# Dynamic convolution and squared-ReLU FFN on one core: the convolution of blocks 8 to 32 cut into 64-row pieces in two row halves

## Chip, core and metric

The kernel runs on one core of a Trainium2 chip. The time is device microseconds from the first to the last instruction of one execution with what lies around it; the median of three runs before the change is 729.51 us (729.48 to 729.95). One more execution was recorded by the profiler: its span is 728.4 us.

## What is computed

Every token of 8 sequences of 4096 tokens has 192 channels in 8 heads of 24. For each token and head a softmax over 7 generated weights gives the taps of a causal convolution over this token and the 6 before it. The result goes through an FFN of width 2048 with a squared ReLU.

```python
w = softmax(weight_gen, axis=-1)                       # (8, 4096, 8 heads, 7 taps)
x_pad = concatenate([zeros((B, 6, D)), x], axis=1)     # causal
out[b, s, h] = sum over k of w[b, s, h, k] * x_pad[b, s + k, head h]
y = out.reshape(32768, 192)
result = maximum(y @ w_in, 0) ** 2 @ w_out             # 192 -> 2048 -> 192
```

## The kernel before

Tokens are taken in 64 sub-blocks of 512 (`TB`). The first two are blocks of their own, all others go in pairs, so there are 33 blocks (`BLOCKS`, numbered from 0). From block 8 on (`FIRST_SPREAD`) a block's convolution is `st_conv_spread`; these are 25 blocks, sub-blocks 14 to 63.

**Convolution as matmul.** A sub-block is cut into 5 pieces of 128 tokens (`NT`, `STEP` = 104): a piece starts 24 tokens before the first of its 104 new tokens (96 in the last piece), so that the 6 tokens of history lie in it. `x_load` brings the pieces of x with POOL's DMA queue, 128 tokens on partitions, 192 channels wide, casting to fp16 on the way (`block_load`: one transfer for all 5 pieces, two or three where a piece starts elsewhere). `wr_load` brings the softmax weights of the same tokens from a DRAM buffer on SP's queue in the same cut. `st_band` (DVE) multiplies the weights, repeated along the columns, by a 0/1 mask, which gives for each head a band matrix of 128 rows (tokens read) by 104 columns (tokens made). The matmul takes 32 channels of x as weights (128x32) and a head's band as the moving operand (128x104). `st_conv_spread` runs over 4 head pairs k (three pairs of heads, and a fourth slot that holds the heads left over), 5 pieces, 2 sub-blocks (`half`) and 2 heads (`e`): 80 matmuls. The four of (`half`, `e`) go to the four groups of 32 columns of the array (`tile_position=(0, p0)`) and so to four groups of 32 PSUM partitions. Each result tile `yp` holds two k in two PSUM banks of 512 columns, two tiles a block: ACT evicts the first, DVE the second, to `y` in fp16 (L512). Then four small transfers on SP's queue move the rows of the leftover heads to where the FFN wants them (L516).

**FFN.** `st_unit` makes a 128-wide slice of the hidden layer for both halves: 6 matmuls of 64x512, the two 64-row halves of the array at a time (L581). ACT applies the ReLU (L595), DVE squares (L599). `st_mm2` runs one block later: matmuls with 64x128 weights and 192 columns, again two row halves at a time, into two banks (L630); ACT and DVE add the two banks (L644, L646), and SP stores.

**Order.** It is written out by hand. A block's plan (`steady_spread`) is the string `MuMuuu MuMuuu MuCMuuu MuMuuu`: 16 units `u` of this block, 8 half quarters `M` (32 matmuls each) of the second product of the block before, and at `C` the convolution of the next block, followed by the loads of x for the block after that. `B` steps make bands for the next block before units 1 and 5; `S` and `E` steps do a piece of the softmax of a later batch. `load_rows(j + 2)` at the start of a block, or the last `S` of a softmax part, issues the weight loads. On SP's queue these stand between the output stores and the row moves of L516.

**Buffers.** x has 2 (`p_x`, the two sub-blocks of one block), so a load of x waits for the matmuls of the convolution before; weights have 4 (`p_wr`), bands 3 (`p_bd`). Three slots of two PSUM banks (`ps_h`) go round among `yp` and `h`.

Of the kernel before, what the change touches and what calls it, by code (L numbers as in the profile page):

```python
# [9 lines left out]
def kernel(  # L10
# [26 lines left out]
    nc = tc.nc  # L37
    f32 = mybir.dt.float32
    f16 = mybir.dt.float16

    B, S, D = x.shape
    H, KK = weight_gen.shape[2], weight_gen.shape[3]
# [5 lines left out]
    FIRST_SPREAD = 8  # L48
    HP = H // 2

    P = 128
    TB = 512
    NBB = S // TB
    NSUB = B * NBB
    BLOCKS = [(0, 1), (1, 1)] + [(n, 2) for n in range(2, NSUB, 2)]
# [6 lines left out]
    SL = 8  # L62
    RT = 64
    NK = D // RT

    NT = 5
    STEP = 104
    BASE = -24
    starts = [BASE + STEP * i for i in range(NT)]
    bounds = [0, 104, 208, 312, 416, TB]  # L70
    ROW_ORDER = (0, 1, 2, 3, 4)

    AluOp = mybir.AluOpType
    AxisX = mybir.AxisListType.X
# [2 lines left out]
    const = ctx.enter_context(tc.tile_pool(name="const", bufs=1))  # L77
# [5 lines left out]
    p_bd = ctx.enter_context(tc.tile_pool(name="p_bd", bufs=3))  # L83
# [5 lines left out]
    ps_h = ctx.enter_context(tc.tile_pool(name="ps_h", bufs=3, space=bass.MemoryType.PSUM))  # L89
# [6 lines left out]
    w_p = const.tile([P, WQ, 2, NQ + NQ // 2], f16, name="w_p")  # L96
    w_o = const.tile([P, NF, Dm], f16, name="w_o")
    mask = const.tile([P, P, 2], f16, name="mask")
    FIRST = 8
    NSEL = TB + TB - P + FIRST + P  # L100
    sel = const.tile([P, NSEL], f16, name="sel")
    PARTS = {0: (8, 8, 8, 8), 1: (8, 8, 16), 2: (16, 16)}
    v_big = const.tile([P, R + 2 * HALO, HP, SL, 2], f16, name="v_big")
    v_first = [
        const.tile([P, FIRST + 2 * HALO, HP, SL, 2], f16, name=f"v_first{i}") for i in (0, 1)
    ]
# [5 lines left out]
            fill=1.0, base=FIRST - 1, channel_multiplier=FIRST,  # L112
        )

    def band_mask():

        nc.gpsimd.memset(mask, 1.0)
        flat = mask.rearrange("p c e -> p (c e)")
        for sign, base in ((1, 0), (-1, 2 * KK - 1)):
            nc.gpsimd.affine_select(  # L120
                out=flat, in_=flat, pattern=[[sign, 2 * P]], compare_op=AluOp.is_ge,
                fill=0.0, base=base, channel_multiplier=-2 * sign,
            )

# [64 lines left out]
    class Softmax:  # L191
# [10 lines left out]
        def load(self, eng, cuts=None):  # L202
            r, rh = self.r, self.rh
            self.wg = wg = self.tile(p_wg, p_wg, "wg", HK, "wg8").rearrange(
                "p (r h k) -> p r h k", h=H, k=KK
            )
            base = weight_gen[self.b, self.t0 : self.t0 + r]
            n = P if self.t0 + P * r + HALO <= S or self.b < B - 1 else P - 1

            def src(first, count, parts):  # L210
                return bass.AP(
                    tensor=base.tensor, offset=base.offset + first * HK,
                    ap=[[r * HK, parts], [1, count * HK]],
                )

            if n == P:
                cuts = cuts or (0, rh)
                for lo, hi in zip(cuts, cuts[1:]):
                    eng.dma_start(  # L219
                        out=wg[:, lo:hi].rearrange("p r h k -> p (r h k)"),  # L220
                        in_=src(lo, hi - lo, P),
                    )
            else:
                nc.vector.memset(wg[:, r:rh], 0.0)
                eng.dma_start(
                    out=wg[:, 0:r].rearrange("p r h k -> p (r h k)"), in_=src(0, r, P)
                )
                eng.dma_start(
                    out=wg[0:n, r:rh].rearrange("p r h k -> p (r h k)"), in_=src(r, HALO, n)
                )  # L230
# [56 lines left out]
    vd_t = {}  # L287
# [7 lines left out]
    x_t, wr_t, pr_t, bd_t, yp_t, y_t, g_t, gp_t, t1_t, o_t, o_sb_t = ({} for _ in range(11))  # L295
# [12 lines left out]
    def tile_start(j, i):  # L308

        t1 = (j % NBB + 1) * TB  # L310
        return TB - P if i == NT - 1 and t1 in ends(j // NBB) else starts[i]

    def block_load(j, dst, src, width, eng):
        t0 = (j % NBB) * TB
        first, last = int(t0 == 0), NT
        if first:
            eng.dma_start(out=dst[:, 0], in_=src[0:P, :])  # L317
        a = t0 + tile_start(j, NT - 1)
        if a != t0 + starts[-1]:
            last = NT - 1  # L320
            eng.dma_start(out=dst[:, last], in_=src[a : a + P, :])
        ap = rows(src, t0 + starts[first], width)
        ap = bass.AP(
            tensor=ap.tensor, offset=ap.offset,
            ap=[ap.ap[0], [STEP * width, last - first], ap.ap[2]],
        )
        eng.dma_start(out=dst[:, first:last], in_=ap)  # L327

    def x_load(j):
        x_t[j] = p_x.tile([P, NT, D], f16, name="xt")  # L330
        block_load(j, x_t[j], x[j // NBB], D, nc.gpsimd)

    def x_load_f32(j):
# [13 lines left out]
    def wr_load(j):  # L347
        wr_t[j] = p_wr.tile([P, NT, HP, SL * 2], f16, name="wr")
        wr = wr_t[j].rearrange("p t g c -> p t (g c)")
        block_load(j, wr, vd_t[j // NBB], H * SL, nc.sync)  # L350

    def wr_load_sbuf(j, parts, order, engines):

# [15 lines left out]
    def select_rows(j, s, tiles, places):  # L369
# [4 lines left out]
        for m, i in enumerate(tiles):  # L374
# [6 lines left out]
            for r in range(s.r):  # L381
                c = a + FIRST - 1 - r
                nc.tensor.matmul(
# [12 lines left out]
    def st_band(j, tiles):  # L396
# [21 lines left out]
            op=AluOp.mult,  # L418
        )

    quads = []
    for q in range(D // 32):
        ha, hb = (32 * q) // G, (32 * q + 31) // G
# [22 lines left out]
    def st_conv_first(j):  # L446
# [10 lines left out]
        places += [(q, r0 + 32 * (q - 4), 1) for r0 in (0, RT) for q in (4, 5)]  # L457
        for i in ROW_ORDER:
            lo, b = bounds[i], bounds[i + 1]
# [21 lines left out]
    def st_conv_spread(j):  # L481

        s0, n = BLOCKS[j]
        y = p_y.tile([P, NK + 1, TB], f16, name="y")
        y_t[j] = y
        for ks in ((NK, NK - 1), (0, 1)):
            yp = ps_h.tile([P, 2, TB], f32, name="yp", tag="h")
            k0 = min(ks)
            for k in ks:
                for i in range(NT):  # L490
                    a, b = bounds[i], bounds[i + 1]
                    for half in (0, 1):
                        s = s0 + half
                        hi = a + (STEP if tile_start(s, i) == starts[i] else b - a)
                        bd = bd_t[s][:, H * a : H * hi].rearrange(
                            "p (g c e) -> p g e c", g=HP, e=2
                        )
                        for e in (0, 1):
                            head = 2 * k + e
                            p0 = RT * half + 32 * e  # L500
                            c0 = min(G * head, D - 32)
                            nc.tensor.matmul(  # L502
                                out=yp[p0 : p0 + 32, k - k0, a:b],
                                lhsT=x_t[s][:, i, c0 : c0 + 32],
                                rhs=bd[:, head // 2, e, 0 : b - a],
                                start=True,
                                stop=True,
                                skip_group_check=True,
                                tile_position=(0, p0),
                            )  # L510
            copy = nc.vector.tensor_copy if k0 == 0 else nc.scalar.copy
            copy(out=y[:, k0 : k0 + 2], in_=yp)  # L512
        for p0 in range(0, P, 32):
            head = SPREAD + p0 // 32 % 2
            r0 = p0 + G * head - min(G * head, D - 32)
            nc.sync.dma_start(out=y[p0 + G : p0 + 32, 0:NK], in_=y[r0 : r0 + G, NK])  # L516
# [139 lines left out]
        )  # L656

    def st_bands(j):
        first = int(j % NBB == 0)
        last = NT - int(tile_start(j, NT - 1) != starts[-1])  # L660
        split = 2 if j == BLOCKS[NFIRST][0] else first
        for tiles in (range(first), range(first, split), range(split, last), range(last, NT)):
            if tiles:
                st_band(j, tiles)

    with nc.allow_low_precision("fp16 matmul pipeline"), tc.manual_schedule():
# [3 lines left out]
        for b in range(B):  # L670
            t0 = 0
# [29 lines left out]

        s0, s1, s2 = parts[:3]
        spin(46)
        band_mask()
        s0_cuts = (0, FIRST // 2, FIRST, s0.rh)
        s0.load(nc.sync, s0_cuts)
        w_st = p_wg.tile([P, (R + HALO) * HK], f32, name="w_st", tag="wg")[:, 0 : NQ + NQ // 2]
# [14 lines left out]
        o0, o1, ring = (ps_o, "o0"), (ps_o, "o1"), (ps_h, "h")  # L722
        select_rows(0, s0, ROW_ORDER, (o1, ring, ring, ring, o0))
        copy_rows(0, ROW_ORDER[:2])
        x_cast(0, nc.scalar.copy, 1, 3)
        copy_rows(0, ROW_ORDER[2:])
        x_cast(0, nc.scalar.copy, 3, NT)
        for i in ROW_ORDER:
            st_band(0, (i,))
        select_rows(1, s0, ROW_ORDER, (o1,))  # L730
        copy_rows(1, ROW_ORDER, NT)
# [17 lines left out]
        s2.load(nc.gpsimd)  # L749
        x_load(2)  # L750
        nc.gpsimd.memset(v_big, 0.0)

# [12 lines left out]
        fill = {}  # L767
# [22 lines left out]
        for n, s in enumerate(parts):  # L790
            k = n - min(m for m, p in enumerate(parts) if p.b == s.b)
# [4 lines left out]
        for n, s in enumerate(parts[4:], 4):  # L796
            b, f = s.b, s.fb
            k = n - min(m for m, p in enumerate(parts) if p.b == b)
# [8 lines left out]
        for j in range(len(plans), NBLK - 1):  # L807
            a = BLOCKS[j + 1][0]
# [67 lines left out]
        for j in range(NBLK):  # L876
# [6 lines left out]
            for step in plans[j].split():  # L883
                kind, n = step[0], int(step[1:] or 0)
# [26 lines left out]
        j = NBLK - 1  # L911
# [44 lines left out]
```

## Time and profile before

| what | value |
|---|---|
| median of three runs | 729.51 us |
| span of the profiled execution | 728.4 us |
| PE busy | 722.0 us (99%) |
| DVE busy | 625.8 us (86%) |
| ACT busy | 612.0 us (84%) |
| POOL busy | 98.5 us (14%) |
| convolution matmuls of blocks 8 to 32 (L502) | 2000: 1600 of 104 columns, 400 of 96 |
| granted TensorE clock | 1.000 |

A line such as `L502 PE MATMUL yp<-bd,xt 128*32 128x104 f16` names the source line, the engine, the operation, the tile written and the tiles read, the part of the array in use (rows x columns) and the moving operand (partitions x elements). PE's weight loads have a row of their own, PEld; they run beside matmuls. Matmuls overlap one another, and their ends are modelled, so the time that a stretch of matmuls takes is read from the chain of waits, where each piece ends when the next begins, and not from the mean duration of one.

### The profile page before, as it was taken

The numbers are of one execution on the slowest core, as the hardware profiler recorded it, in microseconds if no ns is written. First come the engines' busy times: TensorE is split into PE (matmuls) and PEld (weight loads), VectorE is DVE, ScalarE is ACT, GpSimd is POOL, SyncE is SP. The second block draws the span as 40 slices with busy tenths as digits, with TensorE's granted clock in tenths as the row PEclk, the third lists the DMA queues.
The fourth block names the chain that finished last, engine by engine and source line by source line (L and its number), as shares of the span: only waits on it lengthen the run. The fifth ranks groups of instructions, "written<-read, shape, count | busy, mean of one in ns | idle before, by whom it ended". The sixth has DMA issues, their size and how long they took to land.

```text
span 728.4 us, 31046 instructions
## 1 busy us (share of the span) xinstructions
PE 722.0 (99%) x14078; PEld 530.1 (73%) x14078; DVE 625.8 (86%) x839; ACT 612.0 (84%) x731; POOL 98.5 (14%) x146
## 2 busy tenths in 40 slices
PE   8999999999999999999999999999999999999998
PEld 5668877777777777777777777777777777777777
DVE  7999997998898998888988888988888988778753
ACT  6998888888888888888888888888888888888883
POOL 7231223411001100011001010010000110001000
PEclk9999999999999999999999999999999999999999
DMA  9664465676245443356432554343544325444112
GB/s 193 128 113 106 82 125 89 128 142 138 78 71 133 99 84 68 75 116 125 83 62 58 135 104 88 66 74 110 114 78 87 57 53 117 67 87 77 30 46 67
DMA packets 126272, 68.30 MB, mean 94 GB/s; under 512 B 85353, under 2 KB 122556, under 8 KB 125628
## 3 DMA queue, kind: packets, MB, share of 16 engines
q0 software_dynamic: 46192, 19.43, 22.9%
q1 hardware_dynamic: 79804, 46.79, 22.5%
q8 instruction: 110, 1.80, 1.1%
q14 instruction: 22, 0.18, 0.1%
q10 hardware_dynamic: 144, 0.10, 0.0%
HBM read 50.18 MB, written 28.70 MB: 108 GB/s over the span
## 4 chain that ended last, share of the span: by engine, by line
PE 98%; DMA 1%; SPq 0%; ACT 0%; issue 0%; ACTq 0%
PE o L630 47%; PE h L581 44%; PE yp L502 4%; PE h L566 2%; PE yp L536 1%; DMA w_st<-in_moe_w_in_dram 1%; SPq L219 0%; PE yp L466 0%; ACT w_i L740 0%; SPq L135 0%; SPq L133 0%; ACT y L476 0%; SPq L327 0%; SPq L317 0%; ACT o_sb L644 0%
## 5 line engine op out<-in xcount | busy, mean ns | idle before, releaser
L595 ACT ACTIVATE t<-h 128x1024 f16<-128x1024 f32 x512 | 496.6, 1027 | 60.1 <-PE h L581 58.4
L630 PEld LDWEIGHTS <-g 64*128 64x128 f16 (+1 forms) x8032 | 344.3, 94 | 55.2 <-issue 2.3
L630 PE MATMUL o<-w_o,g 64*128 64x192 f16 (+1 forms) x8032 | 380.1, 243 | 0.1
L599 DVE TENSOR_TENSOR g<-t 128x2048 f16<-128x2048 f16 (+1 forms) x287 | 307.4, 1105 | 28.7 <-ACT t L595 28.3
L581 PE MATMUL h<-y,w_p 64*128 64x512 f16 x2400 | 291.7, 376 | 0.0
L581 PEld LDWEIGHTS <-w_p 64*128 64x128 f16 x2400 | 113.9, 94 | 94.8
L406 DVE TENSOR_TENSOR bd<-wr,mask 128x4160 f16<-128x4160 f16 (+4 forms) x90 | 149.5, 1685 | 1.2 <-ACT wr L391 1.2
L646 DVE TENSOR_TENSOR o_sb<-o,o_sb 128x384 f32<-128x384 f32 x123 | 68.4, 556 | 61.4 <-ACT o_sb L644 60.3
L327 POOL DMA_DIRECT2D xt<-in_x_dram x63 | 52.6, 838 | 415.4 <-PE yp L502 362.5
L644 ACT COPY o_sb<-o 128x384 f32<-128x384 f32 x129 | 61.6, 477 | 45.7 <-PE o L630 44.4
L581 PE MATMUL h<-y,w_i 64*128 64x512 f16 x576 | 70.5, 376 | 0.0
L581 PEld LDWEIGHTS <-w_i 64*128 64x128 f16 x576 | 30.5, 94 | 21.7 <-issue 1.2
L502 PEld LDWEIGHTS <-xt 128*32 128x32 f16 x2000 | 24.6, 95 | 10.6 <-issue 10.6
L266 DVE TENSOR_TENSOR v_big<-ex,rcp 128x112 f16<-128x112 f32 (+5 forms) x180 | 29.9, 237 | 2.1 <-DMA vd<-v_big 1.1
L512 DVE CAST y<-yp 128x1024 f16<-128x1024 f32 x25 | 30.4, 1218 | 0.0
L502 PE MATMUL yp<-bd,xt 128*32 128x104 f16 (+1 forms) x2000 | 28.4, 210 | 0.0
L244 ACT ACTIVATE ex<-wg 128x560 f32<-128x560 f32 (+5 forms) x40 | 26.3, 659 | 1.2 <-DMA wg<-in_weight_gen_dram 1.2
L251 DVE TENSOR_REDUCE ssum<-ex 128x80 f32<-128x560 f32 (+5 forms) x40 | 25.6, 639 | 1.3 <-ACT ex L244 1.3
L512 ACT CAST y<-yp 128x1024 f16<-128x1024 f32 x25 | 25.2, 1007 | 0.0
L258 DVE RECIPROCAL rcp<-ssum 128x64 f32<-128x64 f32 (+4 forms) x39 | 23.0, 589 | 1.4
L317 POOL DMA_DIRECT2D xt<-in_x_dram x7 | 3.9, 555 | 120.4 <-PE yp L502 109.4
L361 POOL DMA_DIRECT2D wr<-v_first x24 | 13.0, 559 | 24.0 <-DVE v_first L266 23.8
(42 smaller groups left out, 111.9 us busy)
## 6 DMA issues: line engine op xcount, KB each, us to landing
out_dram<-o_sb SPq DMA_DIRECT2D x63, 384.0 KB
xt<-in_x_dram POOLq DMA_DIRECT2D x42, 240.0 KB, 4.9
wg<-in_weight_gen_dram SPq DMA_DIRECT2D x4, 1064.0 KB
xt<-in_x_dram POOLq DMA_DIRECT2D x21, 192.0 KB, 5.0
wr<-vd SPq DMA_DIRECT2D x38, 80.0 KB
vd<-v_big SPq DMA_DIRECT2D x5, 512.0 KB
y<-y SPq DMA_DIRECT2D x100, 24.0 KB
wg<-in_weight_gen_dram SPq DMA_DIRECT2D x3, 616.0 KB
```

What stands on the lines that cost most here:

```text
L244: nc.scalar.activation(out=self.ex[:, lo:hi].rearrange("p r g k e -> p (r g) k e"), in_=self.wg[:, lo:hi].rearrange("p r (g e) k -> p (r g ...
L266: eng.tensor_tensor(out=bass.AP(tensor=v.tensor, offset=v.offset + lo * H * SL + lo % SL * 2 + g * SL * 2, ap=[list(v.ap[0]), [H * SL + 2, ...
L327: eng.dma_start(out=dst[:, first:last], in_=ap)
L406: nc.vector.tensor_tensor(out=bd_t[j][:, H * lo : H * (lo + len(tiles) * n)].rearrange("p (g m c) -> p g m c", g=shape[1], c=2 * SL), in0= ...
L502: nc.tensor.matmul(out=yp[p0 : p0 + 32, k - k0, a:b], lhsT=x_t[s][:, i, c0 : c0 + 32], rhs=bd[:, head // 2, e, 0 : b - a], start=True, sto ...
L512: copy(out=y[:, k0 : k0 + 2], in_=yp)
L581: nc.tensor.matmul(out=h[:, half], lhsT=w_in_chunk(w, u, slot, half), rhs=y_t[j][r0 : r0 + RT, k], start=(slot == 0), stop=(slot == NK - 1 ...
L595: nc.scalar.activation(out=t1[:, e], in_=h, func=ActF.Relu)
L599: nc.vector.tensor_tensor(out=g[:, a : e + 1], in0=t1[:, a : e + 1], in1=t1[:, a : e + 1], op=AluOp.mult)
L630: nc.tensor.matmul(out=oo[:, cc * Dm : (cc + 1) * Dm], lhsT=g[r0 : r0 + n, cc * P : (cc + 1) * P], rhs=w_o[r0 : r0 + n, fc, :], start=(fc ...
L644: nc.scalar.copy(out=o_sb, in_=o[0][:, c])
L646: nc.vector.tensor_tensor(out=o_sb, in0=o[1][:, c], in1=o_sb, op=AluOp.add)
```

## The change

Sub-blocks from 14 on (`FIRST_HALF`, the first of block 8) are cut differently. Each is split in two halves of 256 tokens; a half is cut into 5 pieces of 64 tokens, four with 56 new tokens (the piece starts 8 before them) and a last one with 32 (starting 32 before them). The first token half lies on partitions 0 to 63, the second on 64 to 127, so a tile holds 2 x 5 pieces and is as wide as before.

- `half_load` takes the place of `block_load` for x and for the weights: for each half one transfer of 4 pieces and one of the last piece. At the start of a sequence 8 rows are cleared by POOL, and one more transfer is issued.
- `half_bands` takes the place of `st_band`: one DVE operation for the four pieces of 56 columns and one for the piece of 32, on all 128 partitions, with a second mask `mask_half`, which POOL makes at the start.
- `st_conv_spread` issues each matmul twice, once for each half, with 64 rows and half as many columns, at `tile_position=(64 r, p0)`. `yp` is laid out as half, k, column, so that each half has a PSUM bank of its own; the evictions read it in the order k, half, column.

```diff
+    HT = TB // 2
+    FIRST_HALF = BLOCKS[FIRST_SPREAD][0]
+    WSTEP = RT - SL
+    windows = [(WSTEP * i, WSTEP * i - SL) for i in range(HT // WSTEP)]
+    windows.append((WSTEP * len(windows), HT - RT))
+    NW = len(windows)
+    w_ends = [a for a, _ in windows[1:]] + [HT]
...
+    def half_load(j, dst, src, width, eng):
+        t0 = (j % NBB) * TB
+        for r in (0, 1):
+            a, p = t0 + HT * r, RT * r
+            first = int(a == 0)
+            if first:
+                nc.gpsimd.memset(dst[0:SL, 0], 0.0)
+                eng.dma_start(out=dst[SL:RT, 0], in_=src[0 : RT - SL, :])
+            eng.dma_start(
+                out=dst[p : p + RT, first : NW - 1],
+                in_=bass.AP(
+                    tensor=src.tensor, offset=src.offset + (a + windows[first][1]) * width,
+                    ap=[[width, RT], [WSTEP * width, NW - 1 - first], [1, width]],
+                ),
+            )
+            b = a + windows[-1][1]
+            eng.dma_start(out=dst[p : p + RT, NW - 1], in_=src[b : b + RT, :])
...
+    def half_bands(j):
+        bd_t[j] = p_bd.tile([P, H * NT * STEP], f16, name="bd")
+        for lo, hi in ((0, NW - 1), (NW - 1, NW)):
+            a, start = windows[lo]
+            n, shift = w_ends[lo] - a, a - start
+            shape = (P, HP * (hi - lo), n // SL, 2 * SL)
+            nc.vector.tensor_tensor(
+                out=bd_t[j][:, H * a : H * w_ends[hi - 1]].rearrange(
...
+                in1=mask_half[:, shift : shift + n]
...
-            yp = ps_h.tile([P, 2, TB], f32, name="yp", tag="h")
+            yp = ps_h.tile([P, 2, 2, HT], f32, name="yp", tag="h")
             k0 = min(ks)
             for k in ks:
-                for i in range(NT):
-                    a, b = bounds[i], bounds[i + 1]
+                for (a, _), b, i in zip(windows, w_ends, range(NW)):
                     for half in (0, 1):
...
-                            nc.tensor.matmul(
-                                out=yp[p0 : p0 + 32, k - k0, a:b],
-                                lhsT=x_t[s][:, i, c0 : c0 + 32],
-                                rhs=bd[:, head // 2, e, 0 : b - a],
...
-                                tile_position=(0, p0),
-                            )
+                            for r in (0, 1):
+                                nc.tensor.matmul(
+                                    out=yp[p0 : p0 + 32, r, k - k0, a:b],
+                                    lhsT=x_t[s][RT * r : RT * (r + 1), i, c0 : c0 + 32],
+                                    rhs=bd[RT * r : RT * (r + 1), head // 2, e],
...
+                                    tile_position=(RT * r, p0),
+                                )
             copy = nc.vector.tensor_copy if k0 == 0 else nc.scalar.copy
-            copy(out=y[:, k0 : k0 + 2], in_=yp)
+            copy(
+                out=y[:, k0 : k0 + 2].rearrange("p k (r c) -> p k r c", r=2),
+                in_=yp.rearrange("p r k c -> p k r c"),
+            )
...
     def st_bands(j):
+        if j >= FIRST_HALF:
+            return half_bands(j)
...
         nc.gpsimd.memset(v_big, 0.0)
+        band_mask(mask_half, RT)
```

`x_load` and `wr_load` call `half_load` from sub-block 14 on, and `band_mask` takes the mask and its number of rows as arguments.

## Prediction

> **What bounds the kernel now.** First the page: busy times, the chain that ended last, and the queue that brings instructions.
>
> ```profile
> PE 722.0 (99%) x14078; PEld 530.1 (73%) x14078; DVE 625.8 (86%) x839; ACT 612.0 (84%) x731; POOL 98.5 (14%) x146
> ...
> q8 instruction: 110, 1.80, 1.1%
> ...
> PE 98%; DMA 1%; SPq 0%; ACT 0%; issue 0%; ACTq 0%
> PE o L630 47%; PE h L581 44%; PE yp L502 4%; PE h L566 2%; PE yp L536 1%; DMA w_st<-in_moe_w_in_dram 1%; SPq L219 0%; PE yp L466 0%; ACT w_i L740 0%; SPq L135 0%; SPq L133 0%; ACT y L476 0%; SPq L327 0%; SPq L317 0%; ACT o_sb L644 0%
> ```
>
> PE alone sets the end: it is 98% of the chain, and no wait for another engine has a share. So the change is worth what it takes from, or adds to, PE's own stream. Whether that stream is bound by columns is read from the chain of waits in a steady stretch.
>
> ```profile
> 392.91 1.94 PE h L581 x18
> 394.86 1.32 PE o L630 x32
> 396.18 0.65 PE h L581 x6
> 396.82 1.08 PE yp L502 x68
> 397.90 1.43 PE o L630 x32
> ```
>
> L581 and L630 run two at a time: 1.94/9 = 215.6 ns a pair of 512 columns, 1.32/16 = 82.5 ns a pair of 192. The line through both is 0.416 ns a column and 2.6 ns a matmul, for each part of the array that works by itself. For the convolution, four at a time, it gives 45.9 ns for a round of 104 columns and 42.5 for 96. A block has 4 k x (4 + 1) rounds: 16 x 45.9 + 4 x 42.5 = 904 ns.
>
> A steady block takes 22.09 us from one convolution to the next (first matmuls at 374.67 and 396.75 in the timeline). 48 pairs of L581 and 128 of L630 are 10.35 + 10.56 = 20.91, so 1.18 us are left for the convolution: 904 ns of columns and 0.27 us around them (the change of tile shape on both sides, the first weight load, jitter). The convolution is bound by columns as well, not by issuing.
>
> Third, the groups with shapes kept apart, for prices:
>
> ```profile
> L406 DVE TENSOR_TENSOR bd<-wr,mask 128x4160 f16<-128x4160 f16 x41 | 94.9, 2316 | 0.0
> ...
> L327 POOL DMA_DIRECT2D xt<-in_x_dram x63 | 52.6, 838 | 415.4 <-PE yp L502 362.5 <-PE yp L536 42.5 <-issue 9.9
> ...
> L406 DVE TENSOR_TENSOR bd<-wr,mask 128x3328 f16<-128x3328 f16 x21 | 39.5, 1882 | 0.0
> ...
> L502 PE MATMUL yp<-bd,xt 128*32 128x104 f16 x1600 | 27.3, 211 | 0.0
> ...
> L317 POOL DMA_DIRECT2D xt<-in_x_dram x7 | 3.9, 555 | 120.4 <-PE yp L502 109.4 <-PE yp L536 11.0
> ```
>
> **PE, the part that counts.** Removed per block: 80 weight loads and 80 matmuls in 20 rounds of four, 904 ns. Added: 160 and 160 in 20 rounds of eight. The 0.27 us around them I leave: the neighbours keep their shapes.
> By columns, a round of 56 takes 0.416 x 56 + 2.6 = 25.9 ns, one of 32 takes 15.9: 16 x 25.9 + 4 x 15.9 = 478 ns, a gain of 426 ns a block, 10.7 us in 25 blocks.
> A round now has 16 instructions, and no row shows PE taking 16 in 26 ns. The nearest short row is the first round of a convolution, a stretch of 14 ns (396.750 to 396.764) with L502's instructions alone:
>
> ```profile
> 396.75:396.76 0.01, 0.01 (x4) 0.01 (x4) 1.00 0.46 55
> ```
>
> Four matmuls and four loads begin in it: 1.75 ns an instruction, so 28 ns for a round of 16, whatever its width. 20 x 28 = 560 ns, a gain of 344 ns a block, 8.6 us in all. The nearest long row is L536 in the window from 48 to 53 us, where 240 instructions take 1.50 us of the chain: 6.25 ns each; but columns bind there too, so it says only that PE can do this much. At that pace 320 instructions take 2.00 us: 1.10 us lost a block, 27.4 us in all. The ends are -10.7 and +27.4 us. I take 28 ns a round: it is PE's own measured pace where nothing but issuing binds, and between a floor of 25.9 and a stream never seen at its limit it is the nearest row.
>
> The Trainium skill (TensorE: Matmul & The Clock Gate, "Wait — 56ns, not 53.3ns?") says that starts are never under about 25 ns apart, however few the columns. Over the whole array 160 matmuls would then need 4.0 us a block; the trace has 80 in 1.08 us, 13.5 ns apart, so the rule can hold at most for each tile. There it would lift the 32-column rounds from 15.9 to 25 ns, an estimate of 514 ns for the block's columns, still under 560.
>
> **DVE.** Rows of 4160 and 3328 elements give 0.522 ns an element and 146 ns a call. Two calls of 1792 and 256 elements: 1081 + 280 = 1.36 us in place of 2.32. Over 50 sub-blocks DVE is busy some 48 us less. Worth nothing: DVE is in no share of the chain. Evictions keep their element counts (ACT 1007 ns, DVE 1218 ns) and read the same banks.
>
> **POOL and x.** Per block 8 transfers in place of 2 to 4, of as many rows. Each 0.56 (L317) to 0.84 us (L327): 4.4 to 6.7 us from the end of the convolution (first issue at 376.10), and 5.0 us, at most 8.0, to landing. Done by 391; needed at 396.75. Cost nothing, covered by the block's 22 us; without this cover every block would wait. The new mask is five small POOL operations at the start, ahead of a load of x that waits for a convolution anyway; the clearing of 8 rows of x waits where its load would.
>
> **SP and the weights.** Also 8 issues in place of 2 or 3. In a steady block they begin at 384.12, and behind them stands an output store that waits for DVE until 394: at L327's median of 0.51 us they end at 388.2. Covered; the row moves of L516, which the next block's first L581 needs, stand before them. At the start of a sequence it is tighter:
>
> ```profile
> 245.14 2.83 SPq L516 DMA_DIRECT2D y<-y  x4
> 248.58 0.34 SPq L280 DMA_DIRECT2D vd<-v_big  x1
> 252.11 0.35 SPq L317 DMA_DIRECT2D wr<-vd  x1
> 252.51 0.97 SPq L327 DMA_DIRECT2D wr<-vd  x2
> 253.59 0.47 SPq L651 DMA_DIRECT2D out_dram<-o_sb  x1
> ```
>
> From 248.92 SP waits for the store to DRAM; then come 9 loads, not 3. The first band of that sub-block is made at 256.17. Its five loads are issued by about 252.1 + 5 x 0.51 = 254.7, and POOL's rows put 3.9 to 5.0 us to landing: DVE may wait up to 3.5 us, some five times in the run. Behind that band stand squares, which the second product needs one block later, and ACT has three buffers of two units ahead. Cost nothing; if the cover failed, 5 x 3.5 = 17 us at most.
>
> **Sum.** 729.5 - 25 x 0.344 = **720.9 us** (the profiled span, 728.4, lies 1.1 us under the median; I take the change from the median).
>
> **Rivals.**
> *Instructions don't come fast enough (slower).* Place: PE's stream in L502. 1.80 MB in 110 packets are 256 instructions of 64 bytes each; 1.1% of 16 engines x 728.4 us over 110 is 1.17 us a packet, 4.6 ns an instruction. A convolution is now 320 instructions in a row, more than a packet. If what is fetched and decoded ahead doesn't carry it, 320 x 4.6 = 1.47 us against 0.904: 0.57 x 25 = +14 us, 743.6. It decides from 904/320 = 2.8 ns an instruction on. For it: today nothing in the trace runs under 5.6 ns for longer than a round. Against it: fetching averages 18% of one engine, and the short row shows 1.75.
> *Gain partly returned.* The same supply at about 2.3 ns: 736 ns a block, -4.2 us, 725.3.
> *Only four at once.* If tiles in the same 32 columns but other row halves take turns: 40 rounds, 32 x 25.9 + 8 x 15.9 = 956 ns, +1.3 us, 730.8: the change doesn't do what it says. For it: no row runs both splits together. Against it: L581 runs row halves and L502 column groups together, each at its line.
> *A transfer is late.* x or the weights arrive after the matmul or band that needs them. At 1 us a block +16, 746. The margins above (5.7 us for x) speak against it.
>
> **Chances.** Forecast (717.9 to 723) 0.48; partly returned (723 to 728) 0.14; four at once 0.10; instruction supply 0.22; transfers 0.06. A measurement here can tell about 0.2% from no change, 1.5 us: 728.0 and 731.0. Faster 0.62; same takes half of four at once, 0.05, and 0.01 of the edges; slower 0.32. The low end is the column floor, 729.5 - 10.7 = 718.8, less 1.3 for switches that may get cheaper between kin shapes: 717.5. The high end takes four at once and the supply rival up to 3.9 ns: 738. Left out are some 0.17. The forecast's own range is 717.9 to 723.
>
> **What would show it.** L502: 4000 matmuls, and per block in the chain 0.65 to 0.8 us in place of 1.08; steady blocks 21.75 us apart. DVE's band rows 1.08 and 0.28 us. POOL's wait for L502 shorter by some 3 us a block, and no PE wait for a transfer of x. I am wrong if the convolution takes over 1.0 us, or if PE shows waits at L502's first matmuls or inside L630 after it.

## The result, and the profile after

| | before | after |
|---|---|---|
| median, four runs each on one chip | 729.73 us (729.48 to 730.99) | 757.65 us (756.0 to 757.89) |
| ratio of the times | 1 | 1.0374, 95% interval 1.0359 to 1.0388 |
| span of the profiled execution | 728.4 us | 755.8 us |

The change makes the kernel 28 us slower; 720.9 was forecast. The page of the changed kernel, in its parts for busy time, DMA queues and the chain that ended last:

```profile
PE 734.2 (97%) x16078; PEld 543.7 (72%) x16078; DVE 579.5 (77%) x875; ACT 612.2 (81%) x731; POOL 171.2 (23%) x305
...
q8 instruction: 125, 2.05, 1.1%
...
PE 96%; issue 2%; DVE 0%; DMA 0%; ACT 0%; SPq 0%
```

PE has 2000 more matmuls and as many more loads, DVE 46 us less work, POOL 73 us more. PE still sets the end: no other engine and no transfer has a share worth a figure. What is new is "issue 2%", time in which PE stood and waited for nothing that the profile shows. The queue that brings instructions moved 15 packets more, 0.25 MB, which is what 4000 more instructions of 64 bytes come to (0.256 MB).

The chain of waits over a steady block of the changed kernel (start us, us, what) shows where PE stood:

```profile
385.39 1.94 PE h L636 x18
387.33 1.32 PE o L685 x32
388.65 0.65 PE h L636 x6
389.30 1.05 PE yp L554 x115
390.35 1.00 issue
391.35 0.49 PE yp L554 x43
391.84 1.43 PE o L685 x32
```

The FFN's pieces are what they were: 1.94, 1.32, 0.65 and 1.43 us. The convolution (now L554) is 2.54 us where it was 1.08, and it is broken by 1.00 us in which PE does nothing. The list of waits of the changed kernel (us in total, times, longest us) says that this is no single event:

```profile
DVE y L564 <- PE yp L554: 34.6, 25, 2.0
PEld L554 <- issue: 27.5, 47, 1.3
PE yp L554 <- issue: 14.3, 19, 1.2
DVE bd L459 <- DMA wr<-vd: 6.9, 5, 1.5
```

DVE, which evicts the second half of the convolution, now waits for PE in all 25 blocks. From the starts of the instructions in the trace, a convolution takes 1.45 to 2.75 us from its first load to the next matmul of L685 (mean 2.14), before 1.05 to 1.10 (mean 1.07). 25 x 1.07 = 26.8 us of the 27.4 us by which the span grew. So nearly all of the loss is in the convolution itself.

Inside one convolution there are three speeds. First the windows of 20 ns from its start, L554 alone (stretch, length, then PE busy and how many matmuls lie in the stretch, PEld busy and how many loads, granted clock, share of the DMA engines, GB/s):

```profile
389.24:389.26 0.02, 0.02 (x8) 0.02 (x11) 1.00 0.00 0
389.26:389.28 0.02, 0.02 (x13) 0.02 (x17) 1.00 0.00 0
389.28:389.30 0.02, 0.02 (x19) 0.02 (x23) 1.00 0.00 0
389.30:389.32 0.02, 0.02 (x24) 0.02 (x29) 1.00 0.00 0
...
389.42:389.44 0.02, 0.02 (x32) 0.02 (x1) 1.00 0.00 0
```

A load lasts about 89 ns, so for the first 89 ns each one that began is still counted: six more in every 20 ns, 3.3 ns a load, 1.7 ns an instruction with its matmul. This is the pace of the row that the prediction took. It ends after 64 instructions (32 loads and 32 matmuls): by 389.43 a single load is under way. In the trace's own starts the instruction at place 65 (places of a convolution are counted from 0) comes 92 ns after the one before. Then the windows of 100 ns, same columns:

```profile
389.80:389.90 0.10, 0.10 (x35) 0.10 (x23) 1.00 0.07 8
389.90:390.00 0.10, 0.10 (x35) 0.10 (x23) 1.00 0.06 8
...
390.30:390.40 0.10, 0.05 (x5) 0.00 (x0) 1.00 0.11 15
391.20:391.30 0.10, 0.00 (x0) 0.00 (x0) 1.00 0.00 0
```

23 loads of 89 ns touch a stretch of 100, so 23 begin in 189 ns: 8.2 ns a load, 4.1 an instruction (in the starts: 25 instructions in 104 or 105 ns, 4.17 each, but for one pause of 30 ns at place 223). The clock granted is 1.00 throughout. At place 232 the stream stops, for 1.18 us from start to start (1.00 us of it is the "issue" of the chain), and then it begins again with 64 instructions at 1.7 ns.

The place of the stop is not the convolution's own. Counted from the first PE instruction of the program, all stops of over 0.2 us in these convolutions lie a multiple of 256 instructions apart, at number 193 of every 256. These are called borders here. A block has 1025 or 1026 instructions, four times 256 and one or two, and so the border moves from place 245 in the first of these convolutions to 215 in the last. A packet of the instruction queue is 16 KB, 256 instructions. The transfers between 388.85 and 389.95 us, in the DMA view of the changed kernel (packets, MB, share of 16 engines in this window):

```profile
q8 instruction: 1, 0.02, 5.7%
```

5.7% of 16 engines x 1.10 us is one packet of 1.00 us, in the trace from 388.90 to 389.90. In the next window, to 391.40, there is none. PE goes on at 391.35, 1.45 us after the packet's end.

### The profile page after: what moved, and what is told of

Read it like the earlier page. It is cut to its first block, busy times and chain, and to the rows that moved or that the text cites. A ratio compares the mean times of both kernels' runs of the same rounds, so it can differ in the third digit from the quotient of the medians.

```text
span 755.8 us, 35511 instructions
## 1 busy us (share of the span) xinstructions
PE 734.2 (97%) x16078; PEld 543.7 (72%) x16078; DVE 579.5 (77%) x875; ACT 612.2 (81%) x731; POOL 171.2 (23%) x305
## 4 chain that ended last, share of the span: by engine, by line
PE 96%; issue 2%; DVE 0%; DMA 0%; ACT 0%; SPq 0%
PE o L685 45%; PE h L636 43%; PE yp L554 5%; PE h L621 2%; PE yp L591 1%; DMA wg<-in_weight_gen_dram 0%; PE pr L414 0%; DVE v_first L275 0%; PE yp L519 0%; DVE rcp L267 0%; ACT w_i L797 0%; DVE ssum L260 0%; ACT y L529 0%; ACT ex L253 0%; SPq L228 0%
## 5 line engine op out<-in xcount | busy, mean ns | idle before, releaser
L685 PEld LDWEIGHTS <-g 64*128 64x128 f16 (+1 forms) x8032 | 345.2, 94 | 53.1 <-issue 2.7
L685 PE MATMUL o<-w_o,g 64*128 64x192 f16 (+1 forms) x8032 | 380.6, 243 | 0.3 <-issue 0.3
L654 DVE TENSOR_TENSOR g<-t 128x2048 f16<-128x2048 f16 (+1 forms) x287 | 311.1, 1106 | 34.4 <-ACT t L650 29.0
L636 PE MATMUL h<-y,w_p 64*128 64x512 f16 x2400 | 292.0, 376 | 0.0
L636 PEld LDWEIGHTS <-w_p 64*128 64x128 f16 x2400 | 115.3, 94 | 93.6
L347 POOL DMA_DIRECT2D xt<-in_x_dram x100 | 66.8, 668 | 339.2 <-PE yp L554 272.3
L636 PE MATMUL h<-y,w_i 64*128 64x512 f16 x576 | 70.7, 376 | 0.0
L459 DVE TENSOR_TENSOR bd<-wr,mask_half 128x1792 f16<-128x1792 f16 x100 | 64.2, 684 | 6.9 <-DMA wr<-vd 6.9
L355 POOL DMA_DIRECT2D xt<-in_x_dram x100 | 58.7, 587 | 0.0
L554 PEld LDWEIGHTS <-xt 64*32 64x32 f16 x4000 | 35.3, 89 | 28.1 <-issue 27.5
L554 PE MATMUL yp<-bd,xt 64*32 64x56 f16 (+1 forms) x4000 | 40.6, 190 | 14.7 <-issue 14.3
L636 PEld LDWEIGHTS <-w_i 64*128 64x128 f16 x576 | 31.6, 94 | 20.8 <-issue 1.2
L437 DVE TENSOR_TENSOR bd<-wr,mask 128x3328 f16<-128x3328 f16 (+5 forms) x26 | 33.0, 1310 | 1.0 <-ACT wr L422 0.7
```

The costliest lines, as they stand in the source:

```text
L347: eng.dma_start(out=dst[p : p + RT, first : NW - 1], in_=bass.AP(tensor=src.tensor, offset=src.offset + (a + windows[first][1]) * width, a ...
L355: eng.dma_start(out=dst[p : p + RT, NW - 1], in_=src[b : b + RT, :])
L437: nc.vector.tensor_tensor(out=bd_t[j][:, H * lo : H * (lo + len(tiles) * n)].rearrange("p (g m c) -> p g m c", g=shape[1], c=2 * SL), in0= ...
L459: nc.vector.tensor_tensor(out=bd_t[j][:, H * a : H * w_ends[hi - 1]].rearrange("p (g m c) -> p g m c", g=shape[1], c=2 * SL), in0=wr_t[j][ ...
L554: nc.tensor.matmul(out=yp[p0 : p0 + 32, r, k - k0, a:b], lhsT=x_t[s][RT * r : RT * (r + 1), i, c0 : c0 + 32], rhs=bd[RT * r : RT * (r + 1) ...
L636: nc.tensor.matmul(out=h[:, half], lhsT=w_in_chunk(w, u, slot, half), rhs=y_t[j][r0 : r0 + RT, k], start=(slot == 0), stop=(slot == NK - 1 ...
```

## The experiments

Three theories at the start. S: the instructions don't come fast enough, by pace and at borders of 256. T: tiles of eight, row halves and column groups together, get in each other's way. L: the new loads, bands or evictions cost it.

**The kernel before, with each convolution matmul cut in two.** No row halves, no new loads or bands, the same columns; only twice the instructions, four tiles at once as before.

```diff
-                for i in range(NT):
+                for i, part in [(i, part) for i in range(NT) for part in (0, 1)]:
                     a, b = bounds[i], bounds[i + 1]
+                    m = (b - a) // 2
...
-                                out=yp[p0 : p0 + 32, k - k0, a:b],
+                                out=yp[p0 : p0 + 32, k - k0, a + m * part : a + m * (part + 1)],
...
-                                rhs=bd[:, head // 2, e, 0 : b - a],
+                                rhs=bd[:, head // 2, e, m * part : m * (part + 1)],
```

> The kernel before, with each convolution matmul of blocks 8 to 32 issued as two of half the columns (52 and 52, or 48 and 48): 160 weight loads and 160 matmuls a block as in the changed kernel, but 128 rows, four column groups, and the old loads, bands and evictions. Theory S (instruction supply: PE takes 64 instructions at 1.7 ns out of its queue, the rest at 4.2 ns each, and waits where the next 256 instructions have not come): the count and the place of the convolution in the program are those of the changed kernel, so the same loss, 757 us (753 to 761), with a pause of about 1 us inside most convolutions. Rival T (row and column tiles hinder each other): columns alone, 32 rounds of 24.2 ns and 8 of 22.6 against 904 ns, +1.4 us, 731. Rival L (the new loads and their waits): 730.

Measured 757.3 us (ratio 1.0381, 1.0357 to 1.0405): the changed kernel's time within 0.4 us. The chain of waits of this run, at the same block:

```profile
388.71 1.07 PE yp L503 x113
389.78 1.15 issue
390.93 0.51 PE yp L503 x43
```

The same three pieces. T and L fall here as causes of the loss: without the row halves and without any of the new transfers, twice the instructions give all of it.

**The changed kernel with 8 columns a matmul.** All 320 instructions stay, but of each half's 256 columns only 40 are computed, and the evictions repeat a few of them; PE has next to nothing to stream.

```diff
-                                    out=yp[p0 : p0 + 32, r, k - k0, a:b],
+                                    out=yp[p0 : p0 + 32, r, k - k0, 8 * i : 8 * i + 8],
...
-                                    rhs=bd[RT * r : RT * (r + 1), head // 2, e],
+                                    rhs=bd[RT * r : RT * (r + 1), head // 2, e, 0:8],
```

> The changed kernel with only the first 8 columns of every convolution matmul of blocks 8 to 32 (56 or 32 before), side by side in PSUM, and an eviction of the same size that repeats them: most of the convolution's columns are left out, all 320 instructions a block stay. Theory S: columns and tiles don't bind, the time stays at 757 (754 to 759). Rival T: fewer columns, so a gain towards a round of 25 ns or less, 500 ns a block, about 720.

Measured 758.06 us (1.0384, 1.0364 to 1.0404). Columns have next to no part in it: the convolutions take 1.40 to 2.77 us (mean 1.99 against 2.14), and two stretches of 3.41 us at half the clock, worth 3.4 us, make up for the 3.9 us that this saves.

**The changed kernel without its second row half.** The matmuls of r = 1 are left out (half of the convolution), and the evictions read the first half twice: 160 instructions a block.

```diff
-                            for r in (0, 1):
+                            for r in (0,):
...
-                in_=yp.rearrange("p r k c -> p k r c"),
+                in_=yp[:, 0].unsqueeze(2).broadcast_to((P, 2, 2, HT)),
```

> The changed kernel without the matmuls of the second token half (r = 1); the evictions read the first half twice, so half of the convolution of blocks 8 to 32 is left out, and loads, bands and evictions stay. 160 instructions a block. Theory S: the first 64 at 1.7 ns, 96 at 4.2: 0.51 us a block and no pause for instructions, 0.4 us under the kernel before: 719.5 us (717 to 724). Rival T (eight tiles at once hinder each other): also fast, 478 ns of columns, 719. Rival L (loads, bands or evictions of the new layout are what costs): the time stays near 757.

Measured 723.6 us (0.9913, 0.9897 to 0.993), with all of the new loads, bands and evictions in place. From the chain of waits of this run:

```profile
371.26 0.75 PE yp L554 x75
372.01 1.43 PE o L685 x32
```

No stop, and 0.75 us. In the starts of the trace the first 64 instructions take 0.20 us: four tiles at once are held by their columns, and rounds of four begin 26 ns apart. The other 96 come at 4.17 ns each. From the first start to the last it is 0.65 us; the rest is the way into the next matmul. Half of the columns still cost 70% of the time of all of them before: the pace binds here too, but 160 instructions fit.

**The borders moved by 160 instructions.** If the stops lie at borders of the instruction stream, other instructions ahead of the convolutions move them. The warm-up at the start (`spin`, matmuls whose result nothing reads) gets 126 matmuls of 57 columns in place of 46 of 156: 7182 columns in place of 7176, and 160 more instructions.

```diff
-        WARM = 156
+        WARM = 57
...
-        spin(46)
+        spin(126)
```

> The changed kernel with 126 warm-up matmuls of 57 columns in place of 46 of 156: the same array time at the start, 160 more PE instructions ahead of everything, nothing else. Theory S with blocks of 256 instructions: the border between two blocks moves from about place 230 of each convolution's 320 instructions to about place 70, and the pause gets longer: some 1.3 us more a block, 790 us (780 to 800). If only the pace of 4.2 ns an instruction mattered, or tiles, or loads: 757 to 758.

Measured 813.05 us (1.1138, 1.1107 to 1.1169): moved, and worse than expected. The chain of waits of this run:

```profile
377.70 1.42 PE yp L554 x153
379.12 0.27 PE o L685 x4
379.39 2.50 issue
381.89 1.56 PE o L685 x28
383.45 3.39 PE h L636 x18
```

The convolution runs through in 1.42 us. The border that the expectation had in mind lies inside it, at place 85 in the first of these blocks and 55 in the last, and PE does not stop there in any block. The stop is at the next border, behind the convolution, in L685, and it is longer. Later in the run, with the drift from block to block, the stop comes back into the convolution's last places (319 to 311). In every block there is one, 1.43 to 2.92 us, 49.7 us in all. And 18 instructions of L636, which take 1.94 us elsewhere, take 3.39 behind it. The windows of this run over that stretch, all engines (after the length: PE, PEld, DVE, ACT and POOL busy with their counts, then the granted clock):

```profile
381.90:382.90 1.00, 1.00 (x25) 1.00 (x26) 0.00 (x0) 0.00 (x0) 1.00 (x3) 0.97 0.87 95
382.90:383.90 1.00, 1.00 (x12) 0.68 (x9) 0.00 (x0) 0.44 (x1) 1.00 (x3) 0.50 1.09 139
383.90:384.90 1.00, 1.00 (x6) 0.36 (x4) 0.93 (x2) 0.17 (x2) 0.43 (x1) 0.50 1.11 136
```

Half the clock, for some 3 us after the stop. The mean granted clock of this execution is 0.979, so 0.021 x 809.4 = 17.0 us went that way. With 49.7 us of stops and the slower pace (below, 8.8 us) that is 75.5 of the 81.0 us by which its span exceeds that of before.

**The kernel before with the same 160 instructions ahead.** The same two lines are changed in the kernel before.

> The kernel before with the same longer start as e3_shift160 (126 warm-up matmuls of 57 columns, 160 more PE instructions). Theory S: a convolution of 160 instructions is never without them, wherever the border stands: 730 us, within 1.5 of the kernel before. If the start itself cost the 55 us that e3_shift160 lost against the changed kernel, this shows it: about 785.

Measured 731.36 us (1.0025, 1.001 to 1.0039). The longer warm-up itself costs some 1.4 us; no stop appears anywhere in the convolutions.

**The borders moved by 48 instructions.** `WARM = 103` and `spin(70)`: the border inside the convolution moves from places 245 to 215 to places 197 to 167.

> The changed kernel with 70 warm-up matmuls of 103 columns in place of 46 of 156: 48 more PE instructions ahead of everything, nothing else. Theory S with blocks of 256 instructions: the border inside each convolution moves from place 215 to 245 of 320 to about 167 to 197, which leaves more time for the next block, so the pauses get shorter: 0.4 to 0.65 us less a block, 744 us (739 to 752); the pace of 4.2 ns stays. If the 83 us that 160 instructions cost came from the longer start alone, this costs some 25 us more: 780. If only the pace mattered: 757.

Measured 741.48 us (1.0167, 1.0145 to 1.0189): 16 us less than the changed kernel from two constants that have nothing to do with the convolution. From the chain of waits of this run:

```profile
382.10 0.65 PE h L636 x6
382.75 1.42 PE yp L554 x157
384.17 1.43 PE o L685 x32
```

19 of its 25 convolutions take 1.42 us with no stop, though a border lies inside each; the other six lose 0.26 to 0.37 us each, only the first of them at a border. This gives the two parts of the loss by themselves. Pace: (1.42 - 1.07) x 25 = 8.8 us. Stops: 19.1 us, summed from start to start over the changed kernel's trace, of which the quick instructions behind each stop win some 1.1 us back: 26.8 - 8.8 = 18.0 us.

**The convolution in two pieces.** If 320 instructions in a row are too many, 160 at two places of a block should not stop. The plan gets a second letter (A for the first PSUM tile's two k, C for the other), and the second band is made two units earlier:

```diff
-        steady_spread = "MuMuuu" * 2 + "MuCMuuu" + "MuMuuu"
+        steady_spread = "MuMuuuMuAMuuuMuCMuuuMuMuuu"
...
-                us = (1, 5)
+                us = (1, 3)
...
+                elif kind == "A" and j + 1 < NBLK:
+                    st_conv_spread(j + 1, 0)
```

> The changed kernel with the convolution issued in two pieces of 160 instructions, the first result tile after unit 5 and the second where the whole stood, with 5 us of the FFN between them; the second band is made two units earlier. All 320 instructions and all transfers of the changed kernel stay. Theory S: a piece takes what the half convolution took in e2_first_half, 0.75 us with its end and 0.09 before it; two are 1.69 us a block against 1.16 in the kernel before, and no pause, since 160 instructions and a full queue outlast most of a fetch: 729.7 + 13 = 743 us (739 to 752). If the total count of instructions, or the transfers, set the loss: 757 or more, since one more change of tile shape is added.

Measured 774.76 us (1.0595, 1.0565 to 1.0625), a miss. The list of waits of this run:

```profile
PE yp L555 <- DVE bd L459: 19.1, 25, 2.2
```

and its chain of waits at the start of a sequence:

```profile
268.01 0.29 DVE bd L459
268.30 1.14 DVE g L657
...
269.46 1.10 DVE bd L459
...
270.61 0.76 PE yp L555 x73
```

The first piece comes four units earlier than the convolution did, and there the band is not ready: 19.1 us of waits, and where they pass 2 us the clock halves again (mean 0.989, 0.011 x 774.8 = 8.5 us). The second pieces all take 0.73 us with no stop, though a border lies inside each of them, at place 84 in the first and 36 in the last. The piece length was right, its place was not, and it is the trace that speaks about the stops, not the total.

**Two pieces, both behind the bands.** The first two units later than in the run before, the second behind the unit where the convolution stood, and 192 more instructions ahead; borders still lie inside every piece, at places 140 to 92 of the first and 84 to 36 of the second (`"MuMuuuMuMuuAuMuMCuuuMuMuuu"`, `WARM = 51`, `spin(142)`).

> As e6_two_pieces, with the first piece after unit 6, where its bands are long made, the second after one unit and two half quarters more, and 192 more PE instructions ahead of everything (142 warm-up matmuls of 51 columns), which by theory S puts the borders of the blocks of 256 where they do least. In e6_two_pieces every second piece took 0.73 us to the next matmul and never paused, while the first pieces stood 0.64 us, at five places over 2 us, waiting for DVE's band. Theory S: without those waits two pieces cost 2 x (0.73 + 0.09) = 1.64 us a block against 1.16 in the kernel before: 729.9 + 12 = 742 us (740 to 749, the upper end with some pauses). If splitting the convolution itself costs what e6_two_pieces lost (45 us): 770 or more.

Measured 753.91 us (1.0331, 1.0314 to 1.0348): right about the pieces, wrong about the time. Of 50 pieces 45 take 0.73 us, with no stop; four take 0.83 to 1.10 and one, at the start of a sequence, 2.48. A steady block takes 22.92 us, 0.83 more than before. The chain of waits of this run, from a first piece to behind a second one:

```profile
386.30 0.73 PE yp L555 x78
387.03 0.75 PE h L639 x6
...
391.62 0.56 DVE o_sb L704
392.17 1.14 DVE y L565
393.32 0.04 issue
393.36 0.80 PE h L639 x5
```

Two pieces of 0.73 in place of 1.07 are 0.39 us. The unit behind the second piece needs a PSUM buffer that DVE is still evicting: in the trace 0.53 us lie between two of its matmuls in place of 0.22, another 0.32. What is left, 0.12, is put down to the change of tile shape, which a block now has twice; no run shows it by itself. So 25 x 0.83 = 20.7 us are in the blocks without any stop; the expectation had left out the last two terms.

## Why the prediction was wrong

**The step that failed** is "I take 28 ns a round: it is PE's own measured pace where nothing but issuing binds". The row under it held eight instructions in 14 ns. They came out of a queue that had filled while PE finished the piece before, and that holds 64: the changed kernel's windows show 64 at 1.7 ns and then 4.17. Its first rounds do begin 27 ns apart, as read; behind them a round of 16 is not 28 ns but 67, and the 20 rounds are 1.31 us from the first start to the last where no stop lies among them (the 741 us run), not 0.56. A convolution without a stop goes up by 0.35 us a block where 0.344 less was forecast: +8.8 us in place of -8.6. The Trainium skill (Advanced Engine Details and Errata, "Engine Queue Depths") gives TensorE a queue of 64; the 64 instructions agree with it.

**What was missing altogether** from the sum are the stops, 18 to 19 us. The rival "Instructions don't come fast enough" was the right case, with a chance of 0.22. Its price of 4.6 ns an instruction, from the mean time of a packet, is near the 4.17 measured, and its point of decision, 2.8 ns, was passed. But 743.6 counts a packet's time as an even pace. In fact a block of 256 is used up in one go, and the next seems not to be there yet: with the stops in, the changed kernel's 256 instructions from border to border around a convolution take 2.2 to 3.3 us, and 3.1 to 4.3 in the run with 160 more ahead. In the kernel before, 160 quick instructions and 96 slow ones never took under 3.54 us, and its convolution spends 904/160 = 5.6 ns on an instruction, above the pace. This fits that it shows neither part, wherever the borders lie (the 731.36 us run). How long a block must last can be read closer from the 741.48 us run: its shortest blocks of 256 around a convolution take 2.57 us, and no stop ends them.

The Trainium skill (Runtime: NRT & Kernel Launch, "Instruction fetch mechanics") says that instructions come in blocks of 16 KiB, 256 of them, and that the cost of passing a border is mostly hidden. The packets and the 256 places between stops agree; hidden it is not here, 19.1 us in 25 blocks.

**The upper of the two ends**, +27.4 us from the long row of L536, is by luck the size of the loss. Its 6.25 ns an instruction is no pace of issuing; columns bind there. The range gave this end up at 738, since the row was thought to say nothing of a limit.

**Four at once** is not the case, by the quick start of the convolutions. There rounds of eight tiles begin 27 ns apart in the changed kernel, with 56 columns as with 8. If tiles of the same columns took turns, each round would be two, and in the run without the second row half rounds of four tiles of 56 columns begin 26 ns apart. So the eight tiles do work at once, as the change meant them to; what they gain in columns is lost in instructions.

**What held.** The bands cost what was worked out and stay off the chain; x comes early enough, though POOL issues eight transfers a block; they take 0.67 us (L347) and 0.59 us (L355) each, between the two prices that were taken. From the groups of the changed kernel, shapes kept apart:

```profile
L347 POOL DMA_DIRECT2D xt<-in_x_dram x100 | 66.8, 668 | 339.2 <-PE yp L554 272.3 <-issue 37.3 <-PE h L636 20.9
L459 DVE TENSOR_TENSOR bd<-wr,mask_half 128x1792 f16<-128x1792 f16 x50 | 54.1, 1083 | 6.9 <-DMA wr<-vd 6.9
...
L459 DVE TENSOR_TENSOR bd<-wr,mask_half 128x256 f16<-128x256 f16 x50 | 14.2, 285 | 0.0
```

1083 and 285 ns against 1081 and 280. The wait for weights at a sequence's start came five times, as said, and at most 1.5 us where up to 3.5 was allowed; PE's list of waits has no transfer of x. That all of this costs nothing is shown by the run of before with split matmuls, which has none of it and takes the same time, and by the run without the second row half, which has all of it and takes 723.6 us. The change of tile shape is as before: 304 ns from the last matmul of the unit before it (L581, now L636) to the convolution's first load, in both kernels.

**What stays open.** That the next block is only asked for when a block has been used up, and what the 1.24 to 1.56 us between a packet's end and the first instruction behind a stop are, is read from times alone; no run changed the fetching itself. Nor is it shown what sets the length of a single stop, and why they are longer in the run with 160 more ahead. Other transfers may have a part in it: between 387.50 and 388.85, up to the packet shown above, they keep the 16 DMA engines 88.5% busy. A convolution with only some pieces in row halves, some 224 instructions, was not tried. No kernel here that does the whole convolution beats the one before; the best of the new ones, with the borders moved by 48, is 1.7% slower.

## What to carry to other kernels

A matmul with its load costs PE at least 8.3 ns in a long stream, however small its tile: cutting matmuls so that more tiles work at once pays only as long as a round of n tiles still has n x 8.3 ns of columns, here 67 ns or some 155 columns for eight. Count also the time of any 256 instructions in a row, from border to border. In the kernel before the shortest took 3.54 us, and in the run with 48 more ahead 2.57 us, and neither of these was stopped. Around the convolutions of the changed kernel they would have passed in 1.8 to 2.25 us without the stops, and took 2.2 to 3.3 with them; with 160 more ahead it was 1.2 to 1.85 and 3.1 to 4.3. So some 2.6 us were enough here, and 2.25 were not safe. Where a kernel lies at this limit, some instructions more or less far ahead of the place move its time (here 741, 758 and 813 us with the same convolution), so a comparison of two such kernels says little until their stops have been looked for.

## What the runs showed of the hardware

- At the start of a convolution and behind a stop PE takes some 64 instructions at 1.7 ns each, with tiles of 8 columns or 56, eight at once. Behind them it takes 4.17 ns each at a granted clock of 1.00, with row halves or without. With four tiles of 52 or 56 columns the first 64 take 3.2 ns each, held by columns.
- Eight tiles, two row halves by four column groups, work at once: rounds of eight with 56 columns begin 27 ns apart, rounds of four 26 ns.
- At the border inside a convolution (number 193 of every 256 instructions) PE stood 0 to 1.39 us in the changed kernel; at one border a block it stood 1.43 to 2.92 us in the run with 160 more ahead. The profile gives it as "issue" and names no releaser.
- After a stop the clock can halve: in the run with 160 more ahead all eight stops of 2.06 us and more were followed by some 3 us at 0.50, and two of the 17 shorter ones (1.81 and 1.95 us). The clock's record shows what sets them apart: the halved stretches last 3.41 us each, and their starts lie multiples of 3.41 us apart over the whole run. In this run the clock was halved after every stop that had 1.81 us or more of its time inside one step of this grid, and after none that had 1.63 us or less inside each, such as one of 2.01 us that two steps share. The Trainium skill (TensorE: Matmul & The Clock Gate, "Why this matters for your kernels") advises against PE gaps over about 3 us; here 2.06 us were enough each time.
